# Two regions with chosen start bytes in place of single SBUF tiles, and two groups of writes set behind matmuls

## The chip, the core and the metric

The kernel runs on one core of one Trainium2 chip. The metric is the device time of one execution in microseconds (us); the time quoted for a kernel is the median of its runs.

## The reference

Two blocks stand one behind the other: an attention over channels, and a gated feed-forward block on what it gives. B = 2, N = 6016, C = 256; the second block sees 12032 rows and has 1536 hidden columns.

```python
qn = q / (norm(q, axis=1) + 1e-6);  kn = k / (norm(k, axis=1) + 1e-6)
s  = kn.transpose(0, 2, 1) @ qn / tau          # 256 x 256 for each of 2 batches
a  = softmax(s)
x  = (v @ a).reshape(12032, 256)
xn = x / sqrt(mean(x * x, -1) + 1e-6) * rms_g
g  = xn @ w_gate;  val = xn @ w_val            # 256 -> 1536 each
out = (g * sigmoid(g) * val) @ w_out           # 1536 -> 256
```

## The kernel before

The first 61 us read q and k and form the scores of batch 0 (`scores`, L184), in plain fp32; those of batch 1 are threaded into what follows. From there on all matmuls but these read fp32r operands: every matrix is kept as a high and a low part, and a product is three matmuls (high x high, low x high, high x low).

The 12032 rows are worked off in 24 blocks `j` (0 to 23) of up to 512 rows, and each block in 12 steps `f`, one for 128 of the hidden columns. Blocks 0, 1 and 23 take the direct way (`emit_hidden`, L891 and L907; output in `emit_out`, L944). Blocks 2 to 22 form seven products of half blocks in place of eight (`emit_step`, `product`, L774), and from block 4 on also the output is formed so (`emit_out_turned`, L998). A step of block j is spread over three turns of the loop: its products 5 and 1 are issued as `now`, 3 and 6 one turn later as `mid`, 7, 2 and 4 as `old`. Between product 1 and product 4 of a turn stand the output matmuls (`outs`, a first part `go(0)`), after product 4 their second part `go(1)`. Product 4 adds onto a PSUM bank which VectorE must have read first (L803, `zg` or `zv` <- `pu`, `t`). At the end of an odd turn `round_pair` makes new `gx`, `gy`, `gz`; `run_rounds` (ScalarE, L734) and `run_subs` (GpSimd, L742) write their high and low parts, the `x` part at once and the `y` and `z` parts at the next odd turn (`run_later`).

The order on each engine is the program's order, written out by hand; each engine runs its own queue in order and waits on semaphores for the others. DMAs are issued by SyncE (SP) in the same way.

TensorE has two operands in each matmul: one that stands in the array (loaded by LDWEIGHTS; PEld in the profile) and one that streams through it. In the main stage (`product`, `emit_out_turned`, and `emit_x` at L456) the standing ones are the weights `w`, the sums `s` and `so` and the turned rows `vt`, the streaming ones `xt`, `gx`, `gy`, `gz` and the attention `a`. In blocks 0, 1 and 23 the output matmul L944 has `g` standing and `w` streaming. All are SBUF tiles from pools, each padded to 32 bytes a row. By the program's allocation `xt`, `gx`, `gy`, `gz`, `a` begin at byte 32 past a multiple of 128, and `w`, `s`, `so`, `vt`, `dg`, `iq`, `ident`, `ones` at byte 96. Exceptions: in block 0 `vt` lies in the tiles of `gy` and `gz` (32), for the second half of block 1 in a tile at 32, and in block 23 the hidden rows of steps 0 and 8 (`glast`) lie in the tiles of `vt` (96) while the streaming `w` is at 96 too. A 256-column operand is 1024 bytes a row, so that slices keep these offsets.

`move_v` (L424) transposes v of a block on VectorE into the tile `vw`, which has one buffer in the pool `v_p`. `emit_xT_move` (L534, L543) sends a block's rows through 16 DMAs on SP. `keep_out` stores the output of blocks 0, 1 and 23; for block 1 it is put off (`late`) to the end of step (2, 1) and there copies both halves (L972) into one tile `ob_1` of the pool `so0`, which is not used otherwise until block 3, and issues one DMA (L980).

Of the kernel before, what the change touches and what calls it, by code (L numbers as in the profile page):

```python
# [19 lines left out]
def kernel(  # L20
# [34 lines left out]
    lead = ctx.enter_context(tc.tile_pool(name="lead", bufs=1))  # L55
    const = ctx.enter_context(tc.tile_pool(name="const", bufs=1))
    sw_p = ctx.enter_context(tc.tile_pool(name="sw", bufs=1))
    vt_p = ctx.enter_context(tc.tile_pool(name="vt", bufs=1))
    link = ctx.enter_context(tc.tile_pool(name="link", bufs=1))
# [3 lines left out]
    xt_p = ctx.enter_context(tc.tile_pool(name="xt", bufs=2))  # L63
    g_p = ctx.enter_context(tc.tile_pool(name="g", bufs=1))
    st_p = ctx.enter_context(tc.tile_pool(name="st", bufs=4))
# [12 lines left out]
    ident = const.tile([P, P], F32, tag="ident", name="ident")  # L78
    ones = const.tile([P, P], F32, tag="ones", name="ones")
    half = lead.tile([P, 2 * KC], F32, name="half")  # L80
    mhalf = lead.tile([P, BT], F32, name="mhalf")
    mtau = lead.tile([P, 1], F32, name="mtau")
    g_sb = link.tile([P, KC], F32, name="g_sb")

    WF = KC * 2 * P + C
    w_hl = [const.tile([P, NF, WF], F32R, name=f"w{i}") for i in range(2)]
# [3 lines left out]
    st_p.tile([P, 24], F32, bufs=1, name="even")  # L90

    def f32(ap):
        return ap.bitcast(F32)

# [143 lines left out]
    def norms(b):  # L238
        nrm = st_p.tile([P, 2 * KC], F32, bufs=1, tag="nrm", name=f"nrm_{b}")
        nc.vector.tensor_copy(nrm, pn.pop(b)[:, :2 * KC])  # L240
        nc.gpsimd.tensor_tensor(out=nrm, in0=nrm, in1=half, op=ALU.pow)
        nrms[b] = nrm

    def inverse_norms(b):

        nrm = nrms.pop(b)
        nc.vector.tensor_scalar(
            out=nrm[:, :KC], in0=nrm[:, :KC], scalar1=1e-6, scalar2=None, op0=ALU.add
        )
        nc.vector.tensor_scalar(  # L250
            out=nrm[:, KC:], in0=nrm[:, KC:], scalar1=1e-6, scalar2=mtau,
            op0=ALU.add, op1=ALU.mult,
        )
        iv = st_p.tile([P, 2 * KC], F32, bufs=1, tag="inv", name=f"inv_{b}")
        nc.vector.reciprocal(iv, nrm)
        dg = sw_p.tile([P, KC, P], F32, tag="dg", name=f"dg_{b}")
# [17 lines left out]
    def keep_norms(b):  # L274
        iq = sw_p.tile([P, C], F32, tag="iq", name=f"iq_{b}")
        nc.scalar.activation(out=iq, in_=iqs[b][:, :C], func=AF.Copy)
        iqs[b] = iq
# [3 lines left out]
    def new_z(b):  # L281
        sm_t[b] = (
            sm_p.tile([P, KC, C], F32, tag="z", name=f"z_{b}"),
            st_p.tile([P, 2 * KC], F32, bufs=1, tag="mx", name=f"mx_{b}"),
        )
# [18 lines left out]
    def softmax_div(b, c):  # L304
        if c == 0:
            a_hl[b] = []
            for i in range(2):
                a_hl[b].append(sm_p.tile([P, KC, C], F32R, tag=f"a{i}", name=f"a{i}_{b}"))
# [70 lines left out]
    def new_vT(j, h):  # L379
        if (j, h) == (1, 1):  # L380
            t = xn_p.tile([P, 2, KC, HN], F32R, tag="moved", name=f"vt_{j}_{h}")
            vT[j, h] = [t[:, i] for i in range(2)]
            return
        p, tag = (vt_p, "vt") if j else (g_p, "yz"[h])
        vT[j, h] = [
            p.tile([P, KC, HN], F32R, tag=f"{tag}{i}", name=f"vt{i}_{j}_{h}") for i in range(2)
        ]
# [76 lines left out]
    def emit_x_squares(j, h):  # L464
# [5 lines left out]
        ss = st_p.tile([P, 2], F32, tag="ss", name=f"ss_{j}_{h}")  # L470
# [7 lines left out]
    def emit_rr(j, h):  # L478
# [5 lines left out]
        rr = st_p.tile([P, 2], F32, tag="rr", name=f"rr_{j}_{h}")  # L484
# [16 lines left out]
    def new_xT(j):  # L501
        t = []
        for i in range(2):
            t.append(xt_p.tile([P, XS * HN], F32R, tag=f"xt{i}", name=f"xt{i}_{j}"))
# [143 lines left out]
    so_hl = []  # L648

# [36 lines left out]
    def new_g(tag, n, j, f):  # L686
        return [
            g_p.tile([P, n * HN], F32R, tag=f"{tag}{i}", name=f"g{tag}{i}_{j}_{f}") for i in range(2)
        ]
# [91 lines left out]
    def emit_step(j, f, odd, outs=(), pre=(), mid=()):  # L781
# [65 lines left out]
    spare = {}  # L847

    def last_g(f):

        n = BN
        if 4 <= f < 8:
            if f == 4:
                spare["xt"] = [
                    xt_p.tile([P, XS * HN], F32R, tag=f"xt{i}", name=f"glast{i}") for i in range(2)
                ]
            n = XS * HN // 4
            return [x[:, (f - 4) * n:(f - 3) * n] for x in spare["xt"]]
        if f % 4 < 2:
            p, tag = ((vt_p, "vt"), (sm_p, "a"))[f % 4]  # L860
            return [p.tile([P, n], F32R, tag=f"{tag}{i}", name=f"glast{i}_{f}") for i in range(2)]
# [99 lines left out]
    def keep_out(j, h):  # L961

        if h == 0:
            p, tag = (v_p, "v") if j == NB - 1 else (pool["so0"], "so0") if j else (pool["ob"], "ob")
# [91 lines left out]
    with tc.manual_schedule():  # L1056
# [20 lines left out]
        warm = link.tile([P, 1], F32, tag="warm", name="warm")  # L1077
# [139 lines left out]
        def end_scores():  # L1217
# [6 lines left out]
            for name, n in (("s", 1), ("z", 2), ("wk", 1), ("so0", 1), ("so1", 1)):  # L1224
                pool[name] = ctx.enter_context(tc.tile_pool(name=name, bufs=n, reuse_waits="tile"))
            s_hl.extend(
                pool["s"].tile([P, NP, 3, 2 * P], F32R, name=f"s{i}") for i in range(2)
            )
# [21 lines left out]
        def new_so():  # L1250
            n = 3 * P
            for i in range(2):
                x = pool[f"so{i}"].tile([P, (NS - 1) * n], F32R, tag=f"so{i}", name=f"so{i}")
                so_hl.append([[x[:, k * n:(k + 1) * n]] for k in range(NS - 1)])

        def last_so():

            for x, tag, other in zip(so_hl, ("dg", "iq"), ("ident", "ones")):
                x.append([
                    sw_p.tile([P, 2 * P], F32R, tag=tag, name=f"so_{tag}"),  # L1260
                    const.tile([P, P], F32R, tag=other, name=f"so_{other}"),
# [179 lines left out]
        for i, (j, f) in enumerate(steps):  # L1441
# [8 lines left out]
            if j < WINO or j == NB - 1:  # L1450
# [13 lines left out]
                for o in outs:  # L1464
                    emit_all(o)
            else:
# [49 lines left out]
```

## Time and profile before

| | us |
|---|---|
| median of 3 runs (1249.04 to 1253.53) | 1250.1 |
| profiled execution | 1248.23 |
| its span in the profile | 1246.4 |
| TensorE matmul busy | 1236.0 (99%) |
| weight load busy | 1187.6 (95%) |
| VectorE busy | 1020.9 (82%) |
| ScalarE busy | 862.8 (69%) |
| GpSimd busy | 628.1 (50%) |

Matmuls are pipelined: the duration of one reaches into the next, so that a stream's pace is the distance from start to start, not a duration. In the timeline view neighbouring matmuls of one kind are merged into a row with the start of the first, the time to the end of the last, and a count; the pace comes from the starts of successive rows and their counts.

### The profile page before, as it was taken

Reading aid. Unit: us, or ns where it says so; the run is one execution under the profiler, and the core shown is the slowest. Engines: PE = TensorE matmul, PEld = TensorE weight load, DVE = VectorE, ACT = ScalarE, POOL = GpSimd, SP = SyncE. Lnnn points to the kernel's source line nnn. Section 1 sums busy time; section 2 is a strip of 40 time slices with the busy share of each in tenths; the row PEclk is TensorE's granted clock in tenths of the full one; section 3 lists DMA queues with packets and bytes.
Section 4 is the critical chain, followed back from the end, with each engine's and each line's share of the span. In section 5 each row is a group of like instructions: output and inputs, shape, how many; then the busy total and the mean of one; then the engine's idle time right before and its main releaser. Section 6 shows DMA issues by size and latency. Waiting matters only on the chain.

```text
span 1246.4 us, 25169 instructions
## 1 busy us (share of the span) xinstructions
PE 1236.0 (99%) x9312; PEld 1187.6 (95%) x9312; DVE 1020.9 (82%) x1671; ACT 862.8 (69%) x1769; POOL 628.1 (50%) x530
## 2 busy tenths in 40 slices
PE   9999999999999999999999999999999999999998
PEld 8899988999999999999999999999999999999998
DVE  5789798768978977889988888888889789789773
ACT  5567647677777777876777677677777777776652
POOL 0120256665566466466465465564664664664430
PEclk9999999999999999999999999999999999999999
DMA  8969411120220211211211202202202202101211
GB/s 301 312 228 277 124 34 37 29 39 18 52 35 18 52 30 23 50 19 35 46 23 36 43 16 46 39 14 52 35 18 52 36 18 52 31 19 31 52 35 31
DMA packets 229371, 75.97 MB, mean 61 GB/s; under 512 B 186880, under 2 KB 220800, under 8 KB 229248
## 3 DMA queue, kind: packets, MB, share of 16 engines
q1 hardware_dynamic: 228416, 73.12, 24.7%
q8 instruction: 73, 1.20, 0.4%
q10 hardware_dynamic: 832, 1.25, 0.3%
q14 instruction: 50, 0.41, 0.1%
HBM read 48.50 MB, written 14.42 MB: 50 GB/s over the span
## 4 chain that ended last, share of the span: by engine, by line
PE 89%; DMA 3%; DVE 3%; ACT 2%; issue 1%; POOL 1%; SPq 1%; ACTq 0%; DVEq 0%; POOLq 0%
PE pu L774 41%; PE po L998 25%; PE pq L774 7%; PE px L456 5%; PE s L184 4%; DMA raw<-in_k_dram 3%; PE pg L891 2%; PE pv L891 2%; PE po L944 2%; SPq L543 1%; DVE wk L639 1%; POOL gz L742 1%; POOL gy L742 0%; DVE zh L907 0%; DVE zg L803 0%
## 5 line engine op out<-in xcount | busy, mean ns | idle before, releaser
L774 PE MATMUL pu<-xt,w 128*128 128x256 f32 x2268 | 388.8, 280 | 1.0 <-DVE zv L803 0.6
L774 PE MATMUL pu<-xt,s 128*128 128x256 f32 x2268 | 349.5, 280 | 0.3
L774 PEld LDWEIGHTS pu<-xt,w 128*128 128x128 f32 x2268 | 324.8, 188 | 11.7 <-DVE zv L803 2.4
L742 POOL TENSOR_TENSOR gy<-zg,gy 128x512 fp32r<-128x512 f32 x126 | 168.9, 1341 | 323.0 <-ACT gy L734 296.7
L774 PEld LDWEIGHTS pu<-xt,s 128*128 128x128 f32 x2268 | 308.3, 188 | 10.0 <-ACT zg L837 0.6
L815 ACT ACTIVATE t<-pu 128x512 f32<-128x512 f32 x252 | 150.9, 599 | 102.2 <-DVE zv L804 51.0
L998 PE MATMUL po<-gx,w 128*128 128x256 f32 (+1 forms) x984 | 189.6, 313 | 0.0
L822 DVE TENSOR_TENSOR zg<-zg,zv 128x768 f32<-128x768 f32 x126 | 167.4, 1329 | 10.6
L734 ACT ACTIVATE gx<-zg 128x768 fp32r<-128x768 f32 (+1 forms) x126 | 95.8, 760 | 104.8 <-DVE zg L831 78.6
L998 PEld LDWEIGHTS po<-gx,w 128*128 128x128 f32 x984 | 140.3, 188 | 4.1
L803 DVE TENSOR_TENSOR zg<-pu,t 128x512 f32<-128x512 f32 x126 | 86.3, 685 | 55.3 <-PE pu L774 21.6
L774 PE MATMUL pq<-xt,w 128*128 128x256 f32 x756 | 129.3, 279 | 0.0
L742 POOL TENSOR_TENSOR gz<-zg,gz 128x512 fp32r<-128x512 f32 x76 | 128.1, 1686 | 0.0
L810 ACT ACTIVATE t<-pu 128x256 f32<-128x256 f32 x252 | 95.5, 379 | 38.1 <-PE pu L774 37.2
L774 PEld LDWEIGHTS pq<-xt,w 128*128 128x128 f32 x756 | 106.1, 188 | 0.0
L819 ACT ACTIVATE zg<-zg 128x768 f32<-128x768 f32 x126 | 105.7, 839 | 0.0
L803 DVE TENSOR_TENSOR zv<-pu,t 128x512 f32<-128x512 f32 x126 | 84.4, 670 | 13.6 <-ACT zg L837 6.3
L184 PE MATMUL s<-raw 128*128 128x256 f32 x376 | 85.9, 382 | 3.2 <-DMA raw<-in_k_dram 3.2
L742 POOL TENSOR_TENSOR gx<-zg,gx 128x512 fp32r<-128x512 f32 x50 | 65.4, 1307 | 40.8 <-ACT gx L734 37.9
L998 PE MATMUL po<-gy,w 128*128 128x512 f32 x300 | 84.8, 392 | 0.0
L184 PEld LDWEIGHTS s<-raw 128*128 128x128 f32 x376 | 69.9, 191 | 14.2 <-DMA raw<-in_k_dram 3.9
L734 ACT ACTIVATE gy<-zg 128x512 fp32r<-128x512 f32 x126 | 80.2, 637 | 1.1 <-PE po L998 1.1
(175 smaller groups left out, 2288.9 us busy)
## 6 DMA issues: line engine op xcount, KB each, us to landing
v<-in_v_dram SPq DMA_DIRECT2D x84, 128.0 KB, 3.8
xnT<-xw SPq DMA_DIRECT2D x336, 32.0 KB, 1.9
out_dram<-ob SPq DMA_DIRECT2D x84, 128.0 KB, 3.3
raw<-in_q_dram SPq DMA_DIRECT2D x20, 512.0 KB, 5.1
raw<-in_k_dram SPq DMA_DIRECT2D x19, 512.0 KB, 6.1
wraw<-in_moe_w_gate_dram SPq DMA_DIRECT2D x12, 256.0 KB, 5.8
wraw<-in_moe_w_val_dram SPq DMA_DIRECT2D x12, 256.0 KB, 6.1
wraw<-in_moe_w_out_dram SPq DMA_DIRECT2D x12, 256.0 KB, 6.3
```

The source lines that it names most:

```text
L184: nc.tensor.matmul(out=s_ps[b][:, c, :], lhsT=r[:, 1, t, c * P:(c + 1) * P], rhs=r[:, 0, t, :], start=(t0 + t == 0 and c == 0), stop=(t0 + ...
L456: nc.tensor.matmul(out=px[:, i, :], lhsT=w[:, c, i * P:(i + 1) * P], rhs=x[:, c, :], start=(i == 0 and c == 0 and m == 0), stop=(c == KC - ...
L734: nc.scalar.activation(out=gh, in_=hh, func=AF.Copy)
L742: engine.tensor_tensor(out=gl, in0=hh, in1=f32(gh), op=ALU.subtract)
L774: nc.tensor.matmul(out=out, lhsT=wm[wi], rhs=xm[xi], start=(start and q == 0), stop=(q == 2), skip_group_check=True,)
L803: nc.vector.tensor_tensor(out=z[:, 1:], in0=u, in1=t[:, :2], op=ALU.add)
L810: nc.scalar.activation(out=mt[:, 0], in_=mu[:, 1], func=AF.Copy)
L815: nc.scalar.activation(out=nt[:, 1:], in_=nu, func=AF.Copy)
L819: nc.scalar.activation(out=zg[:, 1:], in_=zg[:, 1:], func=AF.Silu)
L822: nc.vector.tensor_tensor(out=zg[:, 1:], in0=zg[:, 1:], in1=z, op=ALU.mult)
L891: nc.tensor.matmul(out=t[:, :n], lhsT=wgv[wi][:, f, c, wj, :], rhs=x[xi][:, c, :n], start=(m == 0), stop=(m == 3 * KC - 1),)
L998: nc.tensor.matmul(out=acc[b][:, o:o + g.shape[-1]], lhsT=w, rhs=g, start=first, stop=True, skip_group_check=True,)
```

## The change

The tiles of TensorE's operands become slices of three larger allocations. `region` allocates one tile for several operands with 4 spare elements (16 bytes) ahead of the first. The region `still` holds `w` (both parts) and `vt`, the region `moving` holds `a`, `xt` (both turns) and `gx`, `gy`, `gz`, and the region `sums` holds `s` and `so`. `ident`, `ones`, `dg` and `iq` get 16 spare bytes each (`off`), and the small tiles (`smalls`), of 16 bytes padded to 32, are spread between them, so that everything in `moving` begins 16 bytes past a multiple of 128 and everything in `still`, `sums` and the single ones 80. `xn`, `moved`, `v`, `vw` and `z` are tiles as before.

With slices, a new `gx` is no longer a new tile but the same memory. Two groups of writes are therefore set behind the matmuls that still read what they overwrite: in an odd turn `go(1)` of the outputs is issued ahead of `round_pair`, `run_rounds` and `run_subs`, and at step (23, 2) `run_later` comes after `emit_hidden` and the output matmuls, not ahead of them.

`keep_out` for block 1 no longer has the tile in `so0`. Its first half goes into the tile `vw`, its second into `dg` and `iq`, with a DMA each, three in all.

```diff
-    xt_p = ctx.enter_context(tc.tile_pool(name="xt", bufs=2))
-    g_p = ctx.enter_context(tc.tile_pool(name="g", bufs=1))
+    LEAD = 4
+    def region(pool, name, *sizes):
+        t = pool.tile([P, sum(sizes) + 2 * LEAD], F32R, name=name)
+        at = [LEAD + sum(sizes[:i]) for i in range(len(sizes))]
+        return [t[:, a:a + n] for a, n in zip(at, sizes)]
+    def off(name, n):
+        return tiles.tile([P, n + 2 * LEAD], F32, tag=name, name=name)[:, LEAD:LEAD + n]
+    smalls("half", "mhalf")
+    *w_hl, vt0, vt1 = region(tiles, "still", NF * WF, NF * WF, KC * HN, KC * HN)
+    smalls("mtau", "g_sb", "warm")
+    ident = off("ident", P)
...
+    moving = region(
+        tiles, "moving", *[KC * C] * 2, *[XS * HN] * 4, *[n * HN for n in (3, 2, 2) for _ in range(2)]
+    )
+    a_m, xt_m, g_m = moving[:2], [moving[2:4], moving[4:6]], dict(zip("xyz", zip(*[iter(moving[6:])] * 2)))
...
@@ emit_step
                 nc.vector.tensor_tensor(out=zg[:, 0], in0=u[:, 1], in1=zg[:, 0], op=ALU.mult)
+                for go in outs:
+                    go(1)
+                outs = []
                 round_pair(j, f // 2, zg, h)
                 del zs[j, f // 2]
                 run_rounds()
                 run_subs()
...
@@ keep_out
+        if j == 1:
+            dst = out[rows(j), :].rearrange("(p t) e -> p t e", p=P)
+            if h == 0:
+                ob = v_p.tile([P, KC, HN], F32, tag="vw", name="ob_1")
+                nc.scalar.activation(out=ob, in_=o_ps[j][0], func=AF.Copy)
+                nc.sync.dma_start(out=dst[:, :2, :], in_=ob)
+                return
+            for i, ob in enumerate((dg_m, iq_m)):
+                nc.scalar.activation(out=ob, in_=o_ps[j][1][:, i, :], func=AF.Copy)
+                nc.sync.dma_start(out=dst[:, 2 + i, :], in_=ob)
+            return
...
+            *sums, so0, so1 = region(pool["s"], "sums", n, n, *[(NS - 1) * 3 * P] * 2)
...
@@ main loop
-                    if j == NB - 1 and f == 2:
-                        run_later()
                     emit_hidden(j, f, weights.get((j, f), ()))
                 for go in hooks[1]:
                     go()
                 for o in outs:
                     emit_all(o)
+                if j == NB - 1 and f == 2:
+                    run_later()
```

## Rows read from the trace of the kernel before

**Rows 1.** The page: busy time, share and instructions; granted clock in 40 slices.

```profile
PE 1236.0 (99%) x9312; PEld 1187.6 (95%) x9312; DVE 1020.9 (82%) x1671; ACT 862.8 (69%) x1769; POOL 628.1 (50%) x530
PEclk9999999999999999999999999999999999999999
```

**Rows 2.** Waits of TensorE, 320 to 1243 us, longest total: us, times, longest.

```profile
PE pu L774 <- DVE zv L803: 0.6, 3, 0.3
```

**Rows 3.** Timeline of TensorE, block 21: start us, length us, what, count.

```profile
1151.50 0.87 PE L774 MATMUL pu<-xt,s 128*128 128x256 f32 x6
1152.21 0.52 PE L774 MATMUL pu<-xt,w 128*128 128x256 f32 x3
```

**Rows 4.** Timeline of TensorE at 566 us and over a wait at 570.5 us.

```profile
566.85 0.84 PE L774 MATMUL pu<-xt,s 128*128 128x256 f32 x6
567.53 0.50 PE L774 MATMUL pu<-xt,w 128*128 128x256 f32 x3
...
570.25 1.02 PE L774 MATMUL pu<-xt,s 128*128 128x256 f32 x6
571.11 0.52 PE L774 MATMUL pu<-xt,w 128*128 128x256 f32 x3
```

**Rows 5.** Windows of equal length, four blocks apart: us, TensorE busy (count), clock, DMA.

```profile
485.00:520.00 35.00, 35.00 (x287) 1.00 0.20 31
677.00:712.00 35.00, 35.00 (x277) 1.00 0.20 31
```

**Rows 6.** Groups by form, one window each: 350:476, 476:618, 618:1164, 1197:1243.

```profile
L774 PE MATMUL pq<-xt,w 128*128 128x256 f32 x93 | 16.0, 280 | 0.0
...
L774 PE MATMUL pq<-xt,w 128*128 128x256 f32 x108 | 18.3, 278 | 0.0
...
L774 PE MATMUL pq<-xt,w 128*128 128x256 f32 x411 | 70.7, 280 | 0.0
...
L944 PE MATMUL po<-w,glast 128*128 128x256 f32 x108 | 13.7, 281 | 0.0
```

**Rows 7.** Tile px, 60 to 110 us: ns min/median/max of one matmul.

```profile
L456 PE MATMUL px<-a,vt x42: 276/283/466, 61.4 to 98.0; 128*128 128x256 f32 x42
```

**Rows 8.** Timeline of TensorE in the first stage: fp32 scores and warm-up matmuls.

```profile
1.04 2.93 PE L1082 MATMUL warm_first<-ones 128*128 128x128 f32 x12 [1.04 <-DVE ones L1073]
5.73 1.50 PE L1082 MATMUL warm_load<-ones 128*128 128x128 f32 x12
...
19.80 4.48 PE L184 MATMUL s<-raw 128*128 128x256 f32 x20
```

**Rows 9.** Timelines of ScalarE, GpSimd, TensorE at step (23, 2).

```profile
1207.71 0.63 ACT L734 ACTIVATE gy<-zg 128x512 fp32r<-128x512 f32 x1 [1.08 <-PE po L998]
...
1208.55 1.30 POOL L742 TENSOR_TENSOR gy<-zg,gy 128x512 fp32r<-128x512 f32 x1 [1.18 <-PE po L998]
...
1213.98 1.54 PE L998 MATMUL po<-gy,w 128*128 128x512 f32 x6
```

**Rows 10.** Timelines of ScalarE, SP, VectorE, TensorE around the store of block 1.

```profile
202.13 1.08 ACT L972 ACTIVATE ob<-po 128x512 f32<-128x512 f32 x2
...
202.75 10.18 SPq L543 DMA_DIRECT2D xnT<-xw  x16
213.02 0.54 SPq L980 DMA_DIRECT2D out_dram<-ob  x1
216.73 2.44 SPq L350 DMA_DIRECT2D v<-in_v_dram  x4
...
207.47 0.76 DVE L424 STREAM_TRANSPOSE vw<-v 128x256 f32<-128x256 f32 x2
208.15 0.65 DVE L803 TENSOR_TENSOR zg<-pu,t 128x512 f32<-128x512 f32 x1
...
208.49 1.00 PE L774 MATMUL pu<-xt,w 128*128 128x256 f32 x6
```

**Rows 11.** DMA issues: KB each, median us from issue to landing.

```profile
out_dram<-ob SPq DMA_DIRECT2D x1, 512.0 KB, 3.2
```

More of the change, by code (lines that the diff above doesn't have):

```diff
@@ L238, in norms @@
     def norms(b):
-        nrm = st_p.tile([P, 2 * KC], F32, bufs=1, tag="nrm", name=f"nrm_{b}")
+        nrm = small["nrm"]
         nc.vector.tensor_copy(nrm, pn.pop(b)[:, :2 * KC])
@@ L253, in inverse_norms @@
         )
-        iv = st_p.tile([P, 2 * KC], F32, bufs=1, tag="inv", name=f"inv_{b}")
+        iv = small["inv"]
         nc.vector.reciprocal(iv, nrm)
-        dg = sw_p.tile([P, KC, P], F32, tag="dg", name=f"dg_{b}")
+        dg = dg_m.rearrange("p (c n) -> p c n", c=KC)
         for c in range(KC):
@@ L274, in keep_norms @@
     def keep_norms(b):
[L275 removed]
+        iq = iq_m
         nc.scalar.activation(out=iq, in_=iqs[b][:, :C], func=AF.Copy)
@@ L283, in new_z @@
             sm_p.tile([P, KC, C], F32, tag="z", name=f"z_{b}"),
-            st_p.tile([P, 2 * KC], F32, bufs=1, tag="mx", name=f"mx_{b}"),
+            small["mx"],
         )
@@ L305, in softmax_div @@
         if c == 0:
-            a_hl[b] = []
-            for i in range(2):
-                a_hl[b].append(sm_p.tile([P, KC, C], F32R, tag=f"a{i}", name=f"a{i}_{b}"))
+            a_hl[b] = [a.rearrange("p (c n) -> p c n", c=KC) for a in a_m]
         ah, al = a_hl[b]
@@ L383, in new_vT @@
             return
-        p, tag = (vt_p, "vt") if j else (g_p, "yz"[h])
         vT[j, h] = [
-            p.tile([P, KC, HN], F32R, tag=f"{tag}{i}", name=f"vt{i}_{j}_{h}") for i in range(2)
+            x.rearrange("p (c n) -> p c n", c=KC) for x in ((vt0, vt1) if j else g_m["yz"[h]])
         ]
@@ L501, in new_xT @@
     def new_xT(j):
-        t = []
-        for i in range(2):
-            t.append(xt_p.tile([P, XS * HN], F32R, tag=f"xt{i}", name=f"xt{i}_{j}"))
+        t = xt_m[j % 2]
         n = blocks[j][2] * P
@@ L686, in new_g @@
     def new_g(tag, n, j, f):
-        return [
-            g_p.tile([P, n * HN], F32R, tag=f"{tag}{i}", name=f"g{tag}{i}_{j}_{f}") for i in range(2)
-        ]
+        return [g[:, :n * HN] for g in g_m[tag]]
     def by_quarter(t, n, h):
@@ L852, in last_g @@
         if 4 <= f < 8:
[L853 to L856, printed above, removed]
             n = XS * HN // 4
-            return [x[:, (f - 4) * n:(f - 3) * n] for x in spare["xt"]]
+            return [x[:, (f - 4) * n:(f - 3) * n] for x in xt_m[NB % 2]]
         if f % 4 < 2:
-            p, tag = ((vt_p, "vt"), (sm_p, "a"))[f % 4]
-            return [p.tile([P, n], F32R, tag=f"{tag}{i}", name=f"glast{i}_{f}") for i in range(2)]
+            return ((vt0, vt1), a_m)[f % 4]
         x = xn_p.tile([P, 2, n], F32R, tag=("xn", "moved")[f % 2], name=f"glast_{f}")
@@ L1223, in end_scores @@
             phase.close()
-            for name, n in (("s", 1), ("z", 2), ("wk", 1), ("so0", 1), ("so1", 1)):
+            for name, n in (("s", 1), ("z", 2), ("wk", 1)):
                 pool[name] = ctx.enter_context(tc.tile_pool(name=name, bufs=n, reuse_waits="tile"))
-            s_hl.extend(
-                pool["s"].tile([P, NP, 3, 2 * P], F32R, name=f"s{i}") for i in range(2)
-            )
+            n = NP * 3 * 2 * P
+            *sums, so0, so1 = region(pool["s"], "sums", n, n, *[(NS - 1) * 3 * P] * 2)
+            s_hl.extend(x.rearrange("p (f i n) -> p f i n", f=NP, i=3) for x in sums)
+            so_m.extend((so0, so1))
         at(0, NF - 1, lambda: (square(24), add(24)))
@@ L1259, in last_so @@
                 x.append([
-                    sw_p.tile([P, 2 * P], F32R, tag=tag, name=f"so_{tag}"),
-                    const.tile([P, P], F32R, tag=other, name=f"so_{other}"),
+                    tiles.tile([P, n + 2 * LEAD], F32R, tag=t, name=f"so_{t}")[:, LEAD:LEAD + n]
+                    for t, n in ((tag, 2 * P), (other, P))
                 ])
```

50 lines of the change are left out of this document (28 added, 22 removed).

## The prediction

> **What bounds the kernel now.** I read the page first, then the waits of TensorE, then its timeline, windows and groups, and last the engines around the one place where the change makes a new wait. TensorE matmul is busy for 99% of the span and the weight load for 95%, the clock is granted in full in all 40 slices [rows 1], and from 320 us on the largest group of waits that matmuls have is 0.6 us in sum [rows 2]. So nothing that only makes another engine quicker can shorten the kernel. The time is the number of matmuls times their pace, and the pace is where the profile has something to see: it has two values. In block 21 six matmuls of 256 columns go by from 1151.50 to 1152.21 us, 118 ns each [rows 3]. At 566.85 the same six take until 567.53, 113 ns each [rows 4]. The reader should not take this for a difference of work: line, operands and shapes are the same. A pace holds for a long time and changes at a small stall: 113 goes on until 570.25, there six matmuls take 0.86 us, and from 571.11 on the matmuls are 0.02 us longer in groups of three, as in the slow stretch [rows 4]. Two windows of 35 us, four blocks apart, hold 287 matmuls and 277 [rows 5]: 3.5% between the paces.
>
> Where which pace holds is read from the mean duration of one matmul, which is the pace plus some 163 ns (280 goes with 118, 276 with 113). It is 280 in 350 to 476 and in 618 to 1164, 281 from 1197 on, and 278 from 476 to 618, where half of them are at either pace [rows 6]. That makes 126 + 546 + 46 + 71 = 789 us at the slow pace, and I estimate another 80 us of it before 350 us, where fast and slow alternate and fp32 scores are mixed in.
>
> There is a third pace, and it hangs on addresses. In the early stretch the matmuls of `px` have a median duration of 283 ns, which is a pace of 120 [rows 7]; these are chiefly those of block 0 and of the second half of block 1, where the standing `vt` begins at 32 past a multiple of 128, as the streaming `a` does. All others have 64 bytes between the two, and 118 or 113. [...]
>
> **The change, part by part.** *The start bytes.* The distance between what streams and what stands stays at 64; both move 16 bytes down, to a phase of 16 that no operand of the trace before has. Its cost is therefore unknown and gets bounds. From above: every matmul at 120, the pace of equal phases; that is some 2% over 118, on 789 + 80 us, plus 6% on the some 250 us that are fast now, about +30. [...] I take 113 throughout: it is a pace that this distance already shows for hundreds of matmuls on end, and with it what is lost at 118 is gone. Worked out: 3.5% of 789 + 80 us is 30 us. From this comes a small sum of new waits, because at the fast pace TensorE runs closer to VectorE (the waits at 570 us stand in such a stretch [rows 4]); I put 1 us for them, from the 0.6 of [rows 2]. VectorE, ScalarE and GpSimd read and write the same operands at the new start; their cost for that is unknown too, and bounded by their idle shares of 18, 31 and 50% [rows 1]: a few per cent longer would stay hidden.
>
> [...] [rows 7] and [rows 3] show 120 and 118 for the same work at two distances. [...]
>
> *The writes that move.* `go(1)` of an odd turn holds matmuls alone, and the steps that it is moved past (`round_pair`, `run_rounds`, `run_subs`) are ScalarE's and GpSimd's alone. No queue changes its order, no DMA is moved past, and the writers had to wait for the same reads before. Cost 0. At step (23, 2) `run_later` is moved past `emit_hidden` and the outputs. On ScalarE its copy of `gy` stands at 1207.71 after 1.08 us of waiting for the output matmuls; GpSimd ends with `gy` at 1209.85, and TensorE reads it at 1213.98 [rows 9]. The copy now stands behind one Silu and one rounding of ScalarE, about 1 us; 4.1 us of slack hide that. If that cover were gone it would be a stall of about 1 us.
>
> *The store of block 1* is where a new wait comes in, and I count it as a cost. Now ScalarE copies both halves at 202.13, SP first issues the 16 DMAs `xnT<-xw` of block 3, which lie ahead in its queue, until 212.93, and the store at 213.02 [rows 10]; it lands after 3.2 us [rows 11]. Nobody waits for it, as the tile in `so0` is unused. After the change the first half lies in `vw`, which has one buffer, and VectorE writes the next `vw` (block 4, step (2, 3)) at 207.47 [rows 10]. It must then wait for the store to have read it: 213.0 + 3.2 = 216.2, or 8.7 us. Queued behind it on VectorE is L803 of the next turn, at 208.15, and product 4 of that turn adds onto the bank that L803 has to read first; it is in the group of six that starts at 208.49 [rows 10]. TensorE runs in order, so it stands too, almost from the same moment: 8.7 us, of which I take off nothing, since it has 0.16 us of waiting there now. Bounds: 0, if the framework found another place for the tile, and 8.7 plus a slow start of TensorE after the pause. The granted clock is full throughout, but the first 12 warm-up matmuls, which come after TensorE sat idle, take 2.93 us and 12 later ones 1.50 [rows 8]; a start such as that costs 1.4 us. I take 8.7 + 1.4, say 10. Two more issues on SP (0.54 each) lie in its gap from 213.6 to 216.73 [rows 10] and cost nothing.
>
> **Sum**, against the profiled execution of 1248.2: 1248.2 - 30 + 1 + 10 = 1229. The median of the runs is 1.9 us above that execution, within their spread of 4.5, and I forecast on it: 1231.
>
> **The rivals.**
>
> *The phase does nothing and the wait is new (slower).* Pace is then set by the stalls, as now; the long slow stretch stays, and the only thing left of the change is VectorE standing before `vw` at 207 us. For it: the distance of 64 is the same, and within one distance both paces are there, so something other than addresses picks between them. Against it: the 120 of equal phases. Time: 1250.1 + 10 = 1260. It decides as soon as the pace after 618 us is still 118. Without the wait it would be 1250, no change.
>
> *The phase does nothing, but the long stretch falls to the other pace.* The new pause shifts everything after it, and the slow stretch of 546 us that begins at 618 may turn out fast: -3.5% of 546 = -19, +10, so 1241. For it: from 476 to 618 half of the matmuls are at either pace, with nothing but small stalls between [rows 6]. Against it: nothing says that the new pause makes it so.
>
> *The wait isn't there or is hidden.* With the pace at 113, 1221. Against it: one buffer, and SP's order is fixed by the program.
>
> *The new phase is worse:* all matmuls at 120, and the wait: 1250 + 30 + 10 = 1290. For it: an operand that begins at 16 has an odd number of 16-byte pieces ahead of the next multiple of 32, and no row says that this is harmless.
>
> **How the numbers follow.** The forecast (113 throughout, with the wait) 0.43; the wait hidden 0.10; the long stretch falling fast 0.12; no effect and the wait 0.19; no effect without it 0.05; worse phase 0.11. The predicted time is 1231. The range runs from 1215, below the case without the wait and with room for a pace a little under 113, to 1264, which takes in the slower rival; it leaves out the worse phase and a pace near the floor, about 0.17. A difference of 0.5% is about what a measurement of this kernel can tell from none; that is 1244 to 1256. Faster: 0.43 + 0.10 and most of 0.12, 0.60. Same: 0.05 and the rest of 0.12, with some of the mixtures between, 0.12. Slower: 0.28.
>
> **What would show it.** Right: windows of 35 us with about 287 matmuls everywhere, mean durations of 276 in the main stage, no 118 after 618 us; VectorE idle for some 8 us before L424 at about 207 us with a DMA as what ended it, and TensorE idle beside it. Wrong: durations of 280 or more after 618 us; a store of block 1 that VectorE doesn't wait for; VectorE's additions clearly longer than now, or new groups of waits of TensorE over 5 us elsewhere, which would mean that another engine had become the bound.

## The result, and the profile after

The changed kernel takes 1259.45 us (median; 1257.94 to 1260.26) where the kernel before took 1250.1 in the same session (1247.86 to 1253.53): 1.0067 times as long, with a 95% interval of 1.0045 to 1.0089. The profiled execution took 1259.19, of which 1257.3 are its span. The forecast was 1231; what came is inside the range, but on the other side of no change, and it is the time of the first rival, 1260.

The page says as little as that of before [rows 1]: TensorE is busy for 99% of the span, at a full clock but for a dip that the mean of a slice hides (0.997 over the span).

```profile
PE 1241.2 (99%) x9312; PEld 1192.5 (95%) x9312; DVE 1020.3 (81%) x1671; ACT 863.0 (69%) x1770; POOL 628.2 (50%) x530
```

The waits of TensorE have one new row (us in sum, times, longest). In the kernel before, `pu` waited for nothing ahead of 320 us and for 0.6 in its largest row after that [rows 2]:

```profile
PE pu L788 <- DVE zg L817: 8.0, 3, 7.6
```

It is at 209 us. Timelines of SP, VectorE and TensorE there (start, length, what, count, idle time before and what ended it), to be read against [rows 10]:

```profile
202.94 10.18 SPq L558 DMA_DIRECT2D xnT<-xw  x16
213.21 0.53 SPq L978 DMA_DIRECT2D out_dram<-ob  x1
...
207.40 0.42 DVE L845 TENSOR_TENSOR zg<-pu,zg 128x256 f32<-128x256 f32 x1
215.55 0.84 DVE L441 STREAM_TRANSPOSE vw<-v 128x256 f32<-128x256 f32 x2 [7.72 <-DMA out_dram<-ob]
...
208.91 0.52 PE L788 MATMUL pu<-moving,still 128*128 128x256 f32 x3
217.02 1.01 PE L788 MATMUL pu<-moving,still 128*128 128x256 f32 x3 [7.59 <-DVE zg L817]
```

The store of block 1 is issued at 213.21, behind the 16 DMAs `xnT<-xw`; VectorE writes the next `vw` at 215.55, when it has landed, and TensorE stands 7.59 us. Some 5 us into that pause, at 214.4 us, the granted clock falls to 0.50, and until 221.2 it stays there (windows: us, busy and count of TensorE, weight loads, VectorE, ScalarE, GpSimd, then clock, DMA, GB/s):

```profile
216.00:218.00 2.00, 0.98 (x4) 0.98 (x5) 2.00 (x5) 0.59 (x2) 0.00 (x0) 0.50 0.02 4
...
219.00:220.00 1.00, 1.00 (x7) 1.00 (x7) 1.00 (x3) 1.00 (x3) 0.39 (x1) 0.50 0.00 0
...
217.00:222.00 5.00, 4.98 (x24) 4.90 (x25) 4.75 (x9) 3.31 (x7) 2.39 (x2) 0.58 0.00 2
```

The pace is the surprise. The hoped-for 276 ns is nowhere: `pq` has a mean of 280 in 350 to 476, in 476 to 618 and in 618 to 1164 (the answers to [rows 6], by form):

```profile
L788 PE MATMUL pq<-moving,still 128*128 128x256 f32 x93 | 16.0, 280 | 0.0
...
L788 PE MATMUL pq<-moving,still 128*128 128x256 f32 x105 | 18.0, 280 | 0.0
...
L788 PE MATMUL pq<-moving,still 128*128 128x256 f32 x414 | 71.1, 280 | 0.0
```

Yet it isn't the old slow pace either. The two windows of [rows 5], which held 287 matmuls and 277, now hold

```profile
485.00:520.00 35.00, 34.74 (x274) 1.00 0.09 20
677.00:712.00 35.00, 35.00 (x281) 1.00 0.10 20
```

so the fast stretch is lost and the slow one has become a little quicker. The steps from start to start, which do not hang on what work falls into a window, say the same: their means were 113.3 and 117.8 ns in the two windows before and are 117.3 in both now. And the pace no longer holds for long; it goes by the instruction. TensorE's timeline at 800 us:

```profile
800.81 0.86 PE L788 MATMUL pu<-moving,sums 128*128 128x256 f32 x6
801.51 0.51 PE L788 MATMUL pu<-moving,still 128*128 128x256 f32 x3
801.86 1.52 PE L473 MATMUL px<-moving,still 128*128 128x256 f32 x12
```

The twelve of `px`, one standing operand after another from `still`, take (1.52 - 0.28) / 11 = 113 ns each; the six before them, on `sums`, (0.86 - 0.28) / 5 = 116. From 400 to 1100 us all of this averages out. The window of the kernel before,

```profile
400.00:1100.00 700.00, 699.33 (x5608) 1.00 0.19 35
```

and that of the changed one hold the same number of matmuls:

```profile
400.00:1100.00 700.00, 699.42 (x5610) 1.00 0.19 34
```

### The profile page after: what moved, and what is told of

Read it like the earlier page. It is cut to its first block, busy times and chain, and to the rows that moved or that the text cites. A ratio compares the mean times of both kernels' runs of the same rounds, so it can differ in the third digit from the quotient of the medians.

```text
span 1257.3 us, 25177 instructions
## 1 busy us (share of the span) xinstructions
PE 1241.2 (99%) x9312; PEld 1192.5 (95%) x9312; DVE 1020.3 (81%) x1671; ACT 863.0 (69%) x1770; POOL 628.2 (50%) x530
## 4 chain that ended last, share of the span: by engine, by line
PE 89%; DVE 3%; DMA 2%; ACT 2%; SPq 2%; POOL 1%; issue 1%; ACTq 0%; DVEq 0%; POOLq 0%
PE pu L788 40%; PE po L1019 25%; PE pq L788 7%; PE s L204 5%; PE px L473 5%; PE pg L901 3%; PE pv L901 2%; PE po L954 2%; DMA raw<-in_k_dram 2%; SPq L558 1%; POOL moving L756 1%; DVE wk L654 1%; ACT moving L748 0%; DVE zg L817 0%; ACT xn L514 0%
## 5 line engine op out<-in xcount | busy, mean ns | idle before, releaser
L756 POOL TENSOR_TENSOR moving<-zg,moving 128x512 fp32r<-128x512 f32 x252 | 359.2, 1439 | 368.9 <-ACT moving L748 341.5
L788 PE MATMUL pu<-moving,still 128*128 128x256 f32 x2268 | 389.3, 280 | 8.5 <-DVE zg L817 8.0
L788 PE MATMUL pu<-moving,sums 128*128 128x256 f32 x2268 | 350.8, 281 | 0.1
L788 PEld LDWEIGHTS pu<-moving,still 128*128 128x128 f32 x2268 | 325.4, 188 | 19.1 <-DVE zg L817 8.8
L1019 PE MATMUL po<-moving,still 128*128 128x256 f32 (+1 forms) x1512 | 326.4, 324 | 0.0
L788 PEld LDWEIGHTS pu<-moving,sums 128*128 128x128 f32 x2268 | 310.6, 188 | 9.9 <-ACT zg L854 0.4
L748 ACT ACTIVATE moving<-zg 128x512 fp32r<-128x512 f32 (+1 forms) x328 | 221.4, 684 | 119.0 <-DVE zg L845 59.5
L1019 PEld LDWEIGHTS po<-moving,still 128*128 128x128 f32 x1512 | 227.2, 188 | 7.8
L788 PE MATMUL pq<-moving,still 128*128 128x256 f32 x756 | 130.1, 280 | 0.0
L788 PEld LDWEIGHTS pq<-moving,still 128*128 128x128 f32 x756 | 106.5, 188 | 0.0
```

The costliest lines, as they stand in the source:

```text
L748: nc.scalar.activation(out=gh, in_=hh, func=AF.Copy)
L756: engine.tensor_tensor(out=gl, in0=hh, in1=f32(gh), op=ALU.subtract)
L788: nc.tensor.matmul(out=out, lhsT=wm[wi], rhs=xm[xi], start=(start and q == 0), stop=(q == 2), skip_group_check=True,)
L1019: nc.tensor.matmul(out=acc[b][:, o:o + g.shape[-1]], lhsT=w, rhs=g, start=first, stop=True, skip_group_check=True,)
```

## The experiments

Where an operand begins is told modulo 256 here, because that is what turned out to count. The change makes three regions, not the two of the title, and the third, `sums`, is the one that matters. By the programs' own layout, streaming operands, weights (`w`, or `still`) and sums of weights (`s`, `so`, or `sums`) begin at 32, 224 and 224 in the kernel before and at 16, 208 and **80** in the changed one. Modulo 128 the distance is 64 everywhere; modulo 256 it is 192 throughout before (but for the exceptions in blocks 0, 1 and 23), and 192 or 64 after, by whether the matmul stands on a weight or on a sum. The last fourth of the output's sums has tiles of its own, `so_dg`, `so_iq`, `so_ident` and `so_ones`. Before, all four are at 224; after, `so_dg` and `so_ident` are at 80, `so_iq` and `so_ones` at 208.

The table gathers all runs that compute the reference's result. "Matmuls" is TensorE's count in the window from 400 to 1100 us; "pace" is the mean from the start of one matmul of 256 rounded columns to the next start in that window, gaps over 135 ns left out. Ratios are to the kernel before on the same chip.

| kernel | streaming, weights, sums | matmuls | pace, ns | us | ratio (95%) |
|---|---|---|---|---|---|
| before | 32, 224, 224 | 5608 | 117.2 | 1250.1 to 1251.5 | 1 |
| after | 16, 208, 80 | 5610 | 117.2 | 1259.45 | 1.0067 (1.0045 to 1.0089) |
| a_act | 16, 208, 80 | 5611 | 117.2 | 1250.27 | 0.9999 (0.9987 to 1.0011) |
| b_vw | 32, 224, 224 | 5606 | 117.0 | 1260.92 | 1.0085 (1.0056 to 1.0114) |
| a_act_pad | 16, 208, 208 | 5654 | 115.8 | 1242.6 | 0.9936 (0.9912 to 0.996) |
| b_pad | 32, 224, 96 | 5744 | 113.7 | 1230.46 | 0.9839 (0.9816 to 0.9862) |
| a_act_32 | 32, 224, 96 | 5739 | 113.7 | 1230.6 | 0.9837 (0.981 to 0.9863) |
| a_act_32_pad | 32, 224, 224 | 5690 | 114.9 | 1238.17 | 0.9887 (0.9858 to 0.9917) |
| a_act_0 | 0, 192, 64 | 5746 | 113.7 | 1229.89 | 0.9827 (0.9802 to 0.9851) |
| a_32 | 32, 224, 96 | 5742 | 113.6 | 1239.15 | 0.9902 (0.9873 to 0.9931) |
| a_act_48 | 48, 240, 112 | 5610 | 117.2 | 1250.46 | 1.0002 (0.9992 to 1.0012) |
| a_act_32_mv | 160, 224, 224 | 5730 | 113.8 | 1236.87 | 0.9892 (0.9875 to 0.9909) |
| b_pad_wr | 32, 224, 96 | 5747 | 113.7 | 1230.64 | 0.9841 (0.9822 to 0.986) |
| a_act_16_32 | 16, 224, 96 | 5554 | 118.5 | 1259.8 | 1.0077 (1.0053 to 1.01) |
| a_act_32_16 | 32, 208, 80 | 5549 | 118.5 | 1261.47 | 1.0089 (1.0069 to 1.0109) |

after, b_vw and a_32 have the wait at 209 us, the others don't.

**The wait alone.** First it is taken out of the changed kernel (a_act), then put into the kernel before (b_vw).

```diff
-                nc.sync.dma_start(out=dst[:, :2, :], in_=ob)
+                nc.scalar.dma_start(out=dst[:, :2, :], in_=ob)
```

> The changed kernel with one word changed: the store of block 1's first half (the tile in `vw`) is issued by ScalarE instead of SP, so that it no longer stands behind the 16 DMAs `xnT<-xw`. Everything else stays. If the store behind those DMAs is what TensorE stood for, the store is issued at about 203 us, has landed by 206.6, VectorE's write of `vw` at 207.5 finds it done, TensorE's 8.0 us of waits before `pu` and the half clock from 214.4 to 221.2 us are gone, and the time is 1259.5 - 10 = about 1249.5. If the wait had another cause, or is given back later, it stays at 1259. If pauses pick the pace of what follows, the time may land elsewhere, by up to 20 us either way, without a change of addresses.

Measured 1250.27, 9.2 less than the changed kernel. ScalarE issues the store, and VectorE no longer waits for it (timelines of ScalarE's queue and of VectorE):

```profile
204.69 0.36 ACTq L978 DMA_DIRECT2D out_dram<-ob  x1
...
209.35 0.76 DVE L441 STREAM_TRANSPOSE vw<-v 128x256 f32<-128x256 f32 x2
```

The window that showed the low clock in the changed kernel is here

```profile
217.00:222.00 5.00, 5.00 (x40) 4.75 (x39) 4.90 (x8) 4.22 (x10) 4.84 (x6) 1.00 0.46 74
```

TensorE does 40 matmuls in it where the changed kernel did 24: the slow clock cost 16 matmuls, or some 1.9 us at 117, on top of the 7.6. So the wait is all of the loss, and everything else in the change is worth nothing on balance.

The other way round, in the kernel before:

```diff
+        if j == 1:
+            dst = out[rows(j), :].rearrange("(p t) e -> p t e", p=P)
+            if h == 0:
+                ob = v_p.tile([P, KC, HN], F32, tag="vw", name="ob_1")
...
+            for i, tag in enumerate(("dg", "iq")):
+                ob = sw_p.tile([P, C], F32, tag=tag, name=f"ob_1_{tag}")
...
-            p, tag = (v_p, "v") if j == NB - 1 else (pool["so0"], "so0") if j else (pool["ob"], "ob")
+            p, tag = (v_p, "v") if j == NB - 1 else (pool["ob"], "ob")
```

> The kernel before with one part of the change alone: block 1's output goes through `vw`, `dg` and `iq` instead of the unused `so0`, and its store is issued by SP as in the changed kernel. The addresses stay. If this part carries the whole of the loss, VectorE waits for the store near 207 us for some 8 us, TensorE with it, and the time is 1250 + 10 = 1260. If the loss came from the start bytes, it stays near 1250. If a pause re-rolls which of the two paces (113 or 118 ns) the following stretches take, it may also land between 1240 and 1265.

1260.92, or 10.0 more, with this row among TensorE's waits:

```profile
PE pu L774 <- DVE zg L803: 8.1, 2, 7.8
```

The windows of [rows 5] are

```profile
485.00:520.00 35.00, 34.63 (x275) 1.00 0.09 19
677.00:712.00 35.00, 34.90 (x275) 1.00 0.12 24
```

No operand of the main stage moved, and still the first of them, which had 287 matmuls before, is slow now (117.5 ns a step, 113.3 before): the stretches of the two paces lie elsewhere in this execution, and over 400 to 1100 us they came out even. Whether the new pause moved them isn't shown, since one execution of each was traced and the runs of the kernel before differ among themselves by up to 7 us (1246.48 to 1253.71).

**128 bytes ahead of the sums.** The same pad, once in the changed kernel without the wait (a_act_pad), once in the kernel before (b_pad).

```diff
     small["rr3"] = last.tile([P, 2 * KC], F32, name="rr3")
+    last.tile([P, 32], F32, name="pad")
```

> The same, with 128 unused bytes ahead of the region `sums`, so that the sums of weights, too, begin at 208 past a multiple of 256, as `still` does (in the changed kernel they are at 80, and `moving` is at 16). Theory A, the pace hangs on the start addresses modulo 256, and switching between two distances costs extra: with a single distance nearly all matmuls of 256 columns in the main stage go at 113 ns instead of a mean of 117.2, which is 3.3% of some 1000 us, so about 1249.5 - 34 = 1216. Rival B, only the address modulo 128 can matter, or none at all: 128 bytes change nothing, the time is that of the kernel without the pad, about 1249.5, and the mean stays at 117.

1242.6: better by 7.7, where 34 had been expected for one distance and nothing for 128 bytes without effect. The mean is 115.8, neither 113 nor 117.

```diff
     st_p.tile([P, 24], F32, bufs=1, name="even")
+    st_p.tile([P, 32], F32, bufs=1, name="pad")
```

> The kernel before with 128 unused bytes ahead of the sums of weights, so that these begin at 96 past a multiple of 256 while the weights stay at 224 and the streaming operands at 32; modulo 128 nothing changes. Theory A (modulo 256 counts): the long stretches at one pace, 113 or 118 ns, vanish, and the pace goes by the instruction instead, as in the changed kernel, with steps of 119 to 124 ns where matmuls on sums and on weights follow each other; mean 117, time about 1250 to 1256, with the fast stretches of 200 to 350 and 476 to 618 us gone. Rival B (128 bytes are nothing): the stretches stay, time 1250.

1230.46. Both expectations were wrong: with two distances the kernel before is 20 us faster, every run within 1229.89 and 1230.53. Where an operand begins modulo 256 does count, but two distances are not bad as such; at 32 they are good, and at 16 (a_act 1250.27, a_act_pad 1242.6) they are worse than one. That gave a new theory (C): a pace is a standing arrangement of a weight load beside the stream; a pause may start either, and a change of distance between neighbours throws TensorE out of the slow one, if the phase is right.

**Phase and distance crossed.** Four kernels on the code of the change test it: regions that begin 16 bytes later, with two distances (a_act_32) and with one (a_act_32_pad, with the pad above), 16 bytes earlier (a_act_0), and later with the wait left in (a_32). The regions keep their size, so that no other tile moves.

```diff
-    LEAD = 4
+    LEAD = 8
...
-        t = pool.tile([P, sum(sizes) + 2 * LEAD], F32R, name=name)
+        t = pool.tile([P, sum(sizes) + 8], F32R, name=name)
```

> The kernel of a_act with all regions begun 16 bytes later: streaming operands at 32 past a multiple of 256, weights at 224, sums of weights at 96, the very addresses (modulo 256) of b_pad. Only the phase differs from a_act (16, 208, 80). Theory C: a pace is a standing arrangement of a weight load beside the stream; a pause can start either one, and consecutive matmuls on two distances (weights and sums) pull the slow one back to the fast one, but only at a phase of 32 and not of 16. Then nearly all matmuls of 256 columns go at 113 from 350 us on, the mean falls from 117.2 to 113.7, and the time is about 1230. Rival D: b_pad's gain of 20 us came from its own run of pauses and has nothing to do with where operands begin; then this kernel stays at about 1250, as a_act did, with a mixture of paces.

1230.6. Sixteen bytes, with nothing else changed, are worth 20 us, and rival D falls.

> As a_act_32, but with the 128 unused bytes ahead of `sums`, so that weights and sums both begin at 224, one distance to the streaming operands at 32: the addresses of the kernel before. Theory C: without the switches between two distances nothing pulls the slow pace back, long stretches at 113 and at 118 alternate as in the kernel before, time 1235 to 1252, and slower than a_act_32 by at least 5. Rival E, the phase of 32 alone is what is fast in this program: as a_act_32, within 3 us. Rival D: about 1250, the same as a_act_32.

1238.17, from 1233.98 to 1239.38: 7.6 slower than a_act_32, as theory C has it, so rival E falls too. The two timelines show how. Both have a wait of the same kind at 570 us, inside the group of six, and the groups after it are the same. With two distances (a_act_32):

```profile
570.12 1.03 PE L788 MATMUL pu<-moving,sums 128*128 128x256 f32 x6
570.98 0.51 PE L788 MATMUL pu<-moving,still 128*128 128x256 f32 x3
571.33 0.63 PE L1019 MATMUL po<-moving,sums 128*128 128x256 f32 x4
571.80 0.39 PE L1019 MATMUL po<-moving,still 128*128 128x256 f32 x2
572.03 0.50 PE L788 MATMUL pu<-moving,still 128*128 128x256 f32 x3
...
576.79 0.50 PE L788 MATMUL pq<-moving,still 128*128 128x256 f32 x3
577.13 0.50 PE L788 MATMUL pu<-moving,still 128*128 128x256 f32 x3
```

With one (a_act_32_pad):

```profile
570.09 1.01 PE L789 MATMUL pu<-moving,sums 128*128 128x256 f32 x6
570.94 0.52 PE L789 MATMUL pu<-moving,still 128*128 128x256 f32 x3
...
572.00 0.52 PE L789 MATMUL pu<-moving,still 128*128 128x256 f32 x3
...
576.95 0.52 PE L789 MATMUL pq<-moving,still 128*128 128x256 f32 x3
577.30 0.52 PE L789 MATMUL pu<-moving,still 128*128 128x256 f32 x3
```

Three matmuls take 0.50 us at the fast pace (two steps of 113 ns and a duration of 276) and 0.52 at the slow one (two of 118 and 280). After the wait both kernels are above 0.50; the first is back there at 572.03, past three changes between `sums` and `still`, and the second still has 0.52 at 577.30.

But these are not quite the addresses of the kernel before, which took 1251.03 in the same session, 12.9 more than a_act_32_pad. The pad moves `sums` and not the single tiles: `so_dg` and `so_ident` stay at 96, at the other distance of 64, for 6 of the matmuls in a block. They come in two groups a block, and in the second the slow stretch of 570 us ends (a_act_32_pad):

```profile
586.84 0.52 PE L789 MATMUL pu<-moving,still 128*128 128x256 f32 x3
587.20 0.28 PE L1020 MATMUL po<-moving,so_dg 128*128 128x256 f32 x1
...
587.43 0.28 PE L1020 MATMUL po<-moving,so_dg 128*128 128x256 f32 x1
587.55 0.28 PE L1020 MATMUL po<-moving,so_ident 128*128 128x256 f32 x1
...
587.89 0.50 PE L789 MATMUL pu<-moving,sums 128*128 128x256 f32 x3
```

The kernel before, with `so_dg` at 224 like the rest, is as slow behind these matmuls as ahead of them:

```profile
587.01 0.52 PE L774 MATMUL pu<-xt,w 128*128 128x256 f32 x3
587.36 0.28 PE L998 MATMUL po<-gz,so_dg 128*128 128x256 f32 x1
...
588.07 0.52 PE L774 MATMUL pu<-xt,s 128*128 128x256 f32 x3
```

In a_act_32_pad 17 of the 18 slow stretches that begin between 350 and 1150 us end among the matmuls on these tiles. In the kernel before none does, and its stretch from 616 to 1165 us passes them in twelve blocks. This is the clearest sign for theory C: within one kernel, a few matmuls at another distance bring the fast pace back.

> As a_act_32, but with all regions begun 16 bytes earlier than in a_act: streaming operands at 0 past a multiple of 256, weights at 192, sums at 64. If it is the odd multiple of 16 that spoils the switch (16 and 208 are odd multiples, 0 and 32 even ones), this one is as fast as a_act_32, about 1230. If 32 is special, it stays near a_act, 1245 to 1250. Rival D again expects 1250.

1229.89: as fast as at 32, so it isn't 32 that is special.

> The changed kernel with the phase alone undone: regions begin 16 bytes later, at 32, 224 and 96, and block 1's store is issued by SP as in the change, so that the wait at 207 us is back. Theory C: the fast pace is restored after every pause, so the wait costs its 10 us and no more, a_act_32 + 10, about 1240, with the mean pace at 113.7. If pauses decide the pace even with two distances, the stretches after the wait differ from those of a_act_32 and the time is off from that sum by more than 4. Rival D: about 1259, as the changed kernel.

1239.15, 8.6 over a_act_32. The wait costs about what it did in the changed kernel (9.2), and the pace in the window behind it is that of a_act_32 (113.6 and 113.7).

**Another odd phase, and the other distance.** a_act_48 shifts the regions of a_act, and the tiles behind them, by 32 bytes; a_act_32_mv puts the pad ahead of `moving`.

```diff
-    smalls("half", "mhalf")
+    smalls("half", "mhalf", "pad")
```

> The kernel of a_act with 32 unused bytes ahead of the first region: streaming operands at 48 past a multiple of 256, weights at 240, sums at 112, the same distances as in a_act (16) and a_act_32. 48 is an odd multiple of 16 as 16 is. If it is odd multiples of 16 that spoil the return to the fast pace at a change of distance, the mean pace is about 117.2 and the time about 1250, as in a_act. If the phase of 16 is bad for another reason (the first 32 bytes of a line of 64 or 128, say), or 0 and 32 are good for another, this one may be as fast as a_act_32, about 1230.

1250.46, and 5610 matmuls in the window where a_act has 5611: 16 and 48 are alike, 0 and 32 are alike.

```diff
+    tiles.tile([P, 32], F32, name="pad")
     moving = region(
```

> As a_act_32_pad, with the 128 unused bytes ahead of `moving` and thereby ahead of `sums` too: streaming operands at 160 past a multiple of 256, weights and sums both at 224. One distance again, now the other one (the standing operand 64 past the streaming one instead of 192). If one distance alone means that nothing pulls the slow pace back, the stretches of both paces are there again, 1235 to 1252. If it is the distance of 64 between streaming operands and sums that is the fast one, all go at 113, about 1230 or below. The other way round, if 64 is slow by itself, 118 throughout, 1255.

1236.87. In the main stage this is nearly as fast as two distances: a mean of 113.8, and from the first matmul on `so_dg` to the first of block 23 it takes 833.0 us where a_act_32 takes 831.9, a_act_32_pad 839.2 and the kernel before 850.1. The rest of its 6.3 us over a_act_32 lies ahead of the main stage or in the choice of executions (its profiled one is its best, at 1235.62, and that of a_act_32 its worst, at 1233.29). So the distance of 64 is not like that of 192. The table counts pauses in the traces from 350 to 1150 us (steps of 135 ns or more between two matmuls of 256 columns, with the fast pace ahead of them), and those that more than 40 matmuls at the slow pace followed:

| distances | kernel | pauses | followed by over 40 slow matmuls |
|---|---|---|---|
| 192 (64 for 6 matmuls a block) | a_act_32_pad | 21 | 17 |
| 64 (192 for 6 matmuls a block) | a_act_32_mv | 32 | 2 |
| 192 and 64 in turn | a_act_32 | 25 | 0 |
| 192 and 64 in turn | b_pad | 24 | 0 |

And the two slow stretches of a_act_32_mv, again, end among the matmuls on `so_dg` and `so_ident`, which are at 192 there:

```profile
821.16 0.52 PE L789 MATMUL pu<-moving,still 128*128 128x256 f32 x3
821.52 0.28 PE L1020 MATMUL po<-moving,so_dg 128*128 128x256 f32 x1
...
821.76 0.28 PE L1020 MATMUL po<-moving,so_ident 128*128 128x256 f32 x1
...
822.23 0.50 PE L789 MATMUL pu<-moving,still 128*128 128x256 f32 x3
```

So a change either way can end the slow pace, but at 64 a pause seldom starts it. How much of what b_pad and a_act_32 gain comes from the changes and how much from the matmuls at 64 isn't told apart.

**The moved writes.** First put back in a_act_32 (a_act_32_wr), then made alone in b_pad (b_pad_wr).

```diff
                 nc.vector.tensor_tensor(out=zg[:, 0], in0=u[:, 1], in1=zg[:, 0], op=ALU.mult)
-                for go in outs:
-                    go(1)
-                outs = []
                 round_pair(j, f // 2, zg, h)
...
+                    if j == NB - 1 and f == 2:
+                        run_later()
                     emit_hidden(j, f, weights.get((j, f), ()))
...
-                if j == NB - 1 and f == 2:
-                    run_later()
```

> As a_act_32, with the two moved writes put back: the outputs' second half after the rounds again, and the late step of block 23 ahead of the hidden products, as in the kernel before. The sum of the prediction put their move at nothing: then 1230.6 within 1.5 us. If the move cost or gave something, it shows here: the late step was said to have 4.1 us of slack of which it uses about 1, and a stall of 1 us at most if that was wrong.

1590.95, and this doesn't answer the question. With tiles, the next round took a new tile and the outputs kept their old one. A region is written in place, so outputs that are issued after the round read what the round has just written: this kernel computes something else, and its outputs wait for the writes of the round (two rows of its waits):

```profile
POOL moving L756 <- ACT moving L748: 626.1, 152, 11.2
...
PE po L1016 <- ACT moving L748: 174.6, 106, 2.5
```

The move is what regions need. Its price is seen where tiles allow both orders:

> The kernel of b_pad (before, 128 bytes ahead of the sums; tiles, not regions) with the two moved writes of the change alone: the outputs' second half ahead of the rounds, and the late step of block 23 behind the hidden products and the outputs. It computes what the reference wants, since each tile there is taken anew and keeps its readers. Their move was put at nothing in the prediction: then 1230.5, as b_pad, within 1.5 us. If it costs the 1 us of a stall at step (23, 2), 1231.5; if the outputs' matmuls now stand ahead of something that another engine needs, 39 odd turns make that dearer, 1235 and above.

1230.64 beside 1230.46 (ratios 0.9841 and 0.9839): nothing, as forecast, with tiles; within regions it can't be taken apart.

**Which operand.** In all runs so far both kinds of operand moved together. Here 16 bytes move one of them: `lead=4` for `moving` alone with 8 for the rest (a_act_16_32), and the reverse (a_act_32_16).

```diff
-    def region(pool, name, *sizes):
+    def region(pool, name, *sizes, lead=LEAD):
...
+        lead=4
     )
```

> As a_act_32, but the streaming region `moving` alone begins 16 bytes earlier: streaming at 16 past a multiple of 256, weights at 224, sums at 96. If the odd multiple of 16 does its harm in the streaming operand, the mean is near 117.2 and the time near 1250, as in a_act. If it is the standing operand's start that counts, it is as a_act_32, 1230.6. If only the distance between the two counts (now 208 and 80 instead of 192 and 64), anything between is possible, and a_act_32_16 differs from this one.

> The other half: streaming operands at 32 past a multiple of 256, weights at 208 and sums at 80, as in a_act. If the odd multiple of 16 does its harm in the standing operands, about 1250; if in the streaming ones alone, about 1230. If both this and a_act_16_32 are slow, each does it by itself; if both are fast, it takes both together.

1259.8 and 1261.47, a pace of 118.5 in both: both worse than with both odd (a_act, 117.2). So it isn't one operand's start that does the harm. These two differ from the rest in that streaming and standing operands lie an odd multiple of 16 bytes apart (208 and 80, 176 and 48). With an even multiple between them, and weights and sums at two distances, it is 117.2 with both starts odd and 113.7 with both even.

## Why the prediction was wrong

*The start bytes (-30): the step that failed.* "I take 113 throughout: it is a pace that this distance already shows." The distance had been taken modulo 128, from which `sums` and `still` look alike. Modulo 256 the change put them 128 apart, and at a phase of 16 TensorE goes at a mixture of 113 to 124 ns whose mean, 117.2, is by chance that of before. The term measured 0 (a_act, 0.9999). Its bound from above, +30, held: the kernels with other start bytes and no wait lie between some 21 below the kernel before (b_pad, a_act_32, a_act_0) and 10 above it. No run shows the floor that the range of the prediction speaks of; the lowest mean is 113.6. The 113 was picked by the nearest row, and the row was near in the wrong measure: the trace shows what a pace is, but not what an operand's address is modulo 256.

The term was too large as well. Where nearly all matmuls of the main stage do go at 113 (a_act_32, b_pad), the gain is 20, not 30. The prediction counted block 23 and a part of the first 350 us among what is slow and can be gained. Block 23 takes 45.8 us before and 45.7 in a_act_32 and b_pad, and from the first `px` to the first matmul on `so_dg`, at some 350 us, it is 285.3 us before, 286.4 in a_act_32 and 285.0 in b_pad: nothing was gained in either. Of the 0.17 that the prediction puts outside its range only 0.11, the worse phase, is a case in its list.

*The wait (+10): right.* Place, cause, order of queues and both parts of the price came out as worked: 7.6 us of standing (forecast 8.7) and some 1.9 of slow clock (1.4); together 9.2 by a_act, 10.0 by b_vw, 8.6 between a_32 and a_act_32.

*The moved writes (0): right*, by b_pad_wr, as far as tiles can show it. That they could have been left where they were was not claimed, and a_act_32_wr shows that with regions they could not.

*The small waits (+1)* had no pace to follow from and aren't seen.

*The first rival* had the right time, 1260, from the right wait, with a premise that the runs refute: "the phase does nothing". Sixteen bytes changed 1250.27 (a_act) to 1230.6 (a_act_32), and 128 unused bytes changed 1250.89 to 1230.46 (b_pad). The second part of its argument, that pauses pick the pace, fits a_act_32_pad, where slow stretches begin at them. It isn't the whole of it: the long one of before begins at 615.9 us with a step of 123 ns and no pause. The rival of a worse phase had its price of 120 throughout too high: the worst that was found is 118.5.

What stays open is why. That the slow pace is a standing clash of weight load and stream, which a change of distance breaks up at even multiples of 16 and not at odd ones, is a guess of the author's; it fits the kernels of the table with an even multiple of 16 bytes between the operands. That a change of distance ends the slow pace at even multiples is seen in the traces of a_act_32_pad (17 of 18 slow stretches) and a_act_32_mv (both). A clash is not: the profile shows starts and ends of matmuls and weight loads only. Why 64 is less often slow than 192, and why odd multiples are worse, isn't known either. That the other tiles which the pad moves (`zg`, `t`, `wk`) make the difference is unlikely: the pad makes the kernel before faster and a_act_32 slower, and the 16 bytes of a_act_32 move none of them.

## What to carry to other kernels

A matmul-bound kernel can have more than one pace for the same instruction, as this one has (113 and 118 ns); compare start-to-start times of equal matmuls in several stretches before believing that TensorE is at its best. Where two stretches differ, try the layout, which costs a line: here a pad of 128 bytes in the kernel before (b_pad, 1230.46) beats both kernels, as do regions at 0 or 32 without the wait (1229.89 and 1230.6). A start at a multiple of 32 alone is not enough: the kernel before has that, at 1250.1. When two kernels are to have the same layout, list the start of every operand, the small ones too: six matmuls in a block on two such tiles ended 17 of 18 slow stretches here. And when a buffer is given a second use, look up which queue issues the transfer that frees it: nine microseconds hung on 16 unrelated DMAs that stood ahead of it.

## What the runs showed of the hardware

- The mean pace of the same matmuls (256 columns, rounded fp32) was 113.6 to 118.5 ns, over programs that differ in where operands begin modulo 256. With 128 bytes more ahead of the sums it went from 117.2 to 113.7 (before and b_pad), with 16 more ahead of all regions likewise (a_act and a_act_32).
- At a distance of 192 between streaming and standing operands, with starts at 32 and 224, the slow pace lasted for up to 549 us once it had begun (before), and single executions of a kernel differ (1233.98 to 1239.38 in a_act_32_pad; 1246.48 to 1255.21 before, over all sessions). A few matmuls at another distance ended it (17 of 18 slow stretches in a_act_32_pad). With two distances in turn, at a phase of 32, none of 49 pauses was followed by more than 40 matmuls at the slow pace (25 in a_act_32, 24 in b_pad); after the one at 570 us in a_act_32 the fast pace was back at 572.03. The runs lie closer together there (0.6 us in b_pad, 3.4 in a_act_32) and at a phase of 0 (1.4 in a_act_0).
- While TensorE stood for 7.6 us the granted clock fell to 0.50 (after, at 214.4 us); it was at 0.50 in all windows from 216 to 220 us, and from 217 to 222 us TensorE did 24 matmuls where a_act, without the wait, did 40.
